# Another issue order for the first half of a fused attention and feed-forward kernel: values of the fourth pair ahead of the next batch's keys, zero fills moved

## The chip, the core and the metric

The kernel runs on one core of a Trainium2 chip. The core has five engines that run side by side and meet at semaphores: TensorE (PE, with PEld for its weight loads), VectorE (DVE), ScalarE (ACT), GpSimd (POOL) and SyncE (SP). SP mostly issues DMA transfers; ACT issues a few, and POOL issues some through a queue of its own. The metric is the device time of one launch in microseconds (us), lower is better.

## The reference, cut to what matters

```python
# q, k, v: (4 batches, 8 heads, 768 positions, 64)    is_retrieval = [1, 0, 1, 0, 0, 0, 1, 0]
scores = (1 / sqrt(64)) * q @ k.T
causal = rel >= 0                                      # rel = query position - key position
stream = causal & ((key < 4) | (rel < 64))             # 4 sink keys and a window of 64
scores = where(retrieval head ? causal : stream, scores, -1e9)
a = softmax(scores)
x = (a @ v) -> (3072 tokens, 512)                      # heads side by side
h = x @ w_in                                           # w_in: 512 x 2048
g = maximum(h, 0) + alpha * minimum(h, 0)
out = g @ w_out                                        # w_out: 2048 x 512
```

Inputs and output are float32. Three of the eight heads (0, 2, 6) are retrieval heads and see all earlier keys; five are streaming heads.

## The kernel before

The work is tiled by pairs of heads. `PAIRS` is (2, 6), (1, 5), (0, 4), (3, 7), so a batch has four pairs, and the sixteen pairs are numbered n = 0 to 15 (0 to 3 are batch 0, 4 to 7 batch 1, and so on). The feed-forward part works on token tiles t = 0 to 7: each batch is cut into a tile of 512 tokens (even t) and one of 256 (odd t).

The program is not ordered by loops. It defines some 1,070 small items by name, and the string `ORDER` (lines 14 to 71) lists all names once. The loop at line 817 runs them in that order. Each engine executes its own instructions strictly in the order in which they are issued, so `ORDER` fixes the order on PE, DVE, ACT, POOL and SP at once. The names, n being a pair:

- `Lq`, `Lk`, `Lv` n: DMA loads of queries, keys, values (L204 to L249), issued by SP. The buffers qf, kf and vf have four slots each, so pair n uses slot n modulo 4. Rows of queries and retrieval keys of the first two batches are read in long pieces (1,536 bytes, some keys 512); values are always read in rows of 256 bytes (L247, L249).
- `Cq`, `Ck`, `Cv` n: casts to bfloat16 (L320, L333, L348); the letters in `CQ`, `CK` and `CV` (L301 to L303) say on which engine. For n up to 5 most are on POOL. `Cv` of a pair with streaming heads adds copies of the sink rows (L311).
- `Tq`, `Tk`: transposes on PE into a PSUM bank (L363); `tq`, `tk`: copies from there to qT and kT (L368, L386 to L392). From n = 8 on DMA transposes `Dq`, `Dk` do this.
- `S` n.h.m: scores on PE (L411, L421, L428), `s`: their exponential on ACT (L467, L515, L521), `m`: mask factors on DVE. For n below 4 the mask is added on PE instead (L460, L499), with the tiles nmr and nms that POOL makes (items `nmr`, `nms`).
- `A` n.h: weights times values on PE (L554), `a`: division on DVE (L564, L565). `X`, `x`: the transposed result into xT (L579, L584; some by DMA, L573).
- `P` t.f: first feed-forward product (L599), with `p` the relu of the negated value on ACT (L604) and `g` the combination on DVE (L611), which frees the bank. For t = 0 and f below 6 the product comes in three parts, `P0.f.0` (pairs 0 and 1), `.1` (pair 2), `.2` (pair 3).
- `O` t.s.u: quarter u of the second product (L619), `o`: copy out and store (L625, L629). `wi` 0 to 7 and `wo` 0 to 3: the weight loads, issued by POOL (L707, L711). P0.4 and P0.5 need wi2 and wi3, P0.8 to P0.11 wi4 and wi5, P0.12 to P0.15 wi6 and wi7.
- `zero`, `one`, `kz`, `kfz`, `qz`, `vz`, `sz`, `nz`, `ro`, `so`, `vo`: constant fills (L293), on DVE, POOL or ACT (kz2).

PSUM has eight banks. `take` (L145) gives an item the allowed bank that was freed longest ago in the order of issue, `give` (L151) frees it, so the order of issue also decides which earlier item each bank's next user waits for.

Scores of pairs from 4 on are not issued at once: `S` items collect in `burst`, and `emit_burst` (L415) issues them before the next item that may not stand beside a burst (L432). If both heads have at least 576 columns in it, the two heads' matmuls are issued in turns on the two halves of the rows of the array (L428, 64 rows each), otherwise one after the other (L421).

At most eight transfers of SP's and ACT's queues are under way: each transfer waits for the one eight places before it. PE starts with `warm` matmuls on the identity.

Of the kernel before, what the change touches and what calls it, by code (L numbers as in the profile page):

```python
# [11 lines left out]


ORDER = """
Lq0.0 kz3 id zero Lk0 warm0 Ck0.1 qz0 Lk2 La Ck2.0 Lq0.1 vz3 nmr Cq0.0 Cq0.1 vz1 kz0 Lq1 Tq0.0 warm1 Lq2 kz2 Ck0.0
Ck2.1 qz Tk0.0 sz1 sz2 vz0 tq0.0 Cq1 Lk1 warm2 tk0.0 Tk0.1 Lv0 Ck1.0 Cq2 vo S0.0.0 s0.0.0 kz1 tk0.1 Ck1.1 S0.0.2
m6.0.2 Cv0 Tq0.1 m14.0.2 s0.0.2 Lk3 vz2 Tk2 S0.0.1 Lv1 tq0.1 Lq3 Tq1 s0.0.1 tq1 nms Lq5 Ck3.0 S0.1.1 tk2.1 Ck3.1
S0.1.2 Tk1 sz0 s0.1.1 tk2.0 Tq2 S0.1.0 A0.0 Cv1 tk1.0 s0.1.2 S1.0.0 s0.1.0 A0.1 S1.0.1 tq2 s1.0.0 s1.0.1 Lv2 Tk3 wi1
S2.1.1 wi0 so s2.1.1 tk1.1 wi2 S2.1.0 Lk4 a0.0 S1.1.1 s1.1.1 a0.1 X0 Cq3 A1.0 Cv2 Lv3 a1.0 Ck4.1 Lk5 s2.1.0 Cq5 S2.0.2
# [838 lines left out]
```

## Time and profile before

| | |
|---|---|
| median of 4 runs | 233.57 us (231.96 to 234.46) |
| profiled execution | 234.23 us, its span 232.5 us |
| PE busy | 223.1 us (96%), 1998 matmuls |
| DVE, ACT, POOL busy | 152.4, 139.0, 48.6 us |
| chain that ended last | PE 82%, DMA 10% (of these vf 9%), DVE 3% |
| DMA | 36.63 MB, 158 GB/s over the span |
| granted PE clock | 0.999 |

The chain of waits is followed back from the last instruction: at each step to what released it, or to the instruction before it on its engine. In the timeline, a bracket shows how long the engine stood idle before a row and what ended that. Times are counted from the start of the span. A busy PE is not PE at its peak, since matmuls overlap: four matmuls of 512 columns follow each other every 0.216 us (0.86 us for four in the chain), though one alone shows 0.38.

### The profile page before, as it was taken

The page shows a single profiled execution, that of the slowest core. Times are in us where ns is not written, and L with a number is a line of the kernel's source. Part 1 is how long each engine was busy: PE and PEld are TensorE (multiplying, and loading weights), DVE is VectorE, ACT ScalarE, POOL GpSimd, SP SyncE. Part 2 cuts the span into 40 slices and gives each one's busy share as a digit, 9 for nine tenths or more (in the row PEclk, how much of TensorE's full clock was granted, in tenths as well). Part 3 has the DMA queues.
Part 4 walks back from the last instruction along what each step waited for, and adds up shares of the span by engine and source line. Part 5 has one row for each costly group of instructions (what it writes and reads, how often), then busy time and mean ns, then how long its engine had stood idle before and what let it go on. Part 6 is the DMA issues. An engine that isn't in the chain of part 4 may idle for free.

```text
span 232.5 us, 5230 instructions
## 1 busy us (share of the span) xinstructions
PE 223.1 (96%) x1998; PEld 136.4 (59%) x1998; DVE 152.4 (66%) x393; ACT 139.0 (60%) x280; POOL 48.6 (21%) x97
## 2 busy tenths in 40 slices
PE   6989979999999999999999999999999999999994
PEld 5778847556556665665466445556854555554553
DVE  4695746898785865998997358979990345645110
ACT  5578727998698639736764874498522333623231
POOL 3679668001482004000001000010000020000000
PEclk9999999999999999999999999999999999999999
DMA  6989999999999699948989999894310130110033
GB/s 211 274 207 269 234 245 253 202 196 227 223 198 211 143 218 258 231 88 164 196 128 177 239 237 183 160 198 75 71 35 0 45 138 1 45 47 1 0 135 137
DMA packets 92449, 36.63 MB, mean 158 GB/s; under 512 B 79472, under 2 KB 90632, under 8 KB 92424
## 3 DMA queue, kind: packets, MB, share of 16 engines
q1 hardware_dynamic: 86168, 26.97, 56.4%
q0 software_dynamic: 5792, 8.93, 17.4%
q10 hardware_dynamic: 464, 0.40, 0.5%
q8 instruction: 15, 0.25, 0.5%
q14 instruction: 10, 0.08, 0.1%
HBM read 27.55 MB, written 6.29 MB: 146 GB/s over the span
## 4 chain that ended last, share of the span: by engine, by line
PE 82%; DMA 10%; DVE 3%; POOL 1%; SPq 1%; issue 1%; ACT 1%; POOLq 0%; ACTq 0%
PE P L619 35%; PE P L599 33%; DMA vf<-in_v_dram 9%; PE P L554 6%; PE P L428 4%; DVE g L611 2%; PE P L421 2%; PE P L638 2%; DMA kf<-in_k_dram 1%; PE P L579 1%; POOL vb L348 1%; PE P L363 1%; SPq L224 0%; DVE natm L333 0%; ACT neg L604 0%
## 5 line engine op out<-in xcount | busy, mean ns | idle before, releaser
L611 DVE SCALAR_TENSOR_TENSOR g<-neg,oma,P 128x512 bf16<-128x512 f32 (+1 forms) x128 | 72.9, 610 | 38.6 <-ACT neg L604 37.8
L599 PE MATMUL P<-xT,w_in_b 128*128 128x512 bf16 (+1 forms) x512 | 90.1, 326 | 0.0
L619 PE MATMUL P<-w_out_b,g 128*128 128x512 bf16 x368 | 87.6, 379 | 0.0
L604 ACT ACTIVATE neg<-P 128x512 f32<-128x512 f32 x96 | 54.8, 605 | 54.1 <-PE P L599 46.6
L599 PEld LDWEIGHTS <-w_in_b 128*128 128x128 bf16 x512 | 48.9, 98 | 32.2 <-issue 0.2
L619 PEld LDWEIGHTS <-g 128*128 128x128 bf16 x368 | 34.0, 98 | 36.0 <-issue 1.4
L467 ACT ACTIVATE eR<-P 128x448 bf16<-128x448 f32 (+6 forms) x63 | 36.0, 619 | 12.8 <-PE P L460 3.4
L629 POOL DMA_DIRECT2D out_dram<-ot x18 | 9.9, 550 | 127.1 <-ACT ot L625 127.1
L565 DVE TENSOR_TENSOR xn<-P,rcp 128x448 bf16<-128x448 f32 (+1 forms) x32 | 19.4, 608 | 1.1
L625 ACT COPY ot<-P 128x512 f32<-128x512 f32 x23 | 13.3, 595 | 9.1 <-PE P L619 6.7
L515 ACT ACTIVATE eS<-P 128x352 bf16<-128x352 f32 x30 | 13.7, 484 | 5.3 <-PE P L421 4.8
L521 ACT ACTIVATE eS<-P 128x384 bf16<-128x384 f32 (+1 forms) x25 | 13.3, 571 | 5.1 <-PE P L428 2.7
L554 PE MATMUL P<-vb,eS 128*128 128x65 bf16 x260 | 11.3, 193 | 1.7 <-POOL vb L348 1.6
L554 PEld LDWEIGHTS <-eS 128*128 128x128 bf16 x260 | 10.3, 97 | 4.5 <-issue 2.1
L564 DVE RECIPROCAL rcp<-P 128x7 f32<-128x7 f32 (+1 forms) x32 | 6.4, 199 | 8.5 <-PE P L554 8.3
L411 PE MATMUL P<-qT,kT 128*128 128x192 bf16 (+13 forms) x68 | 11.2, 250 | 0.8 <-DVE qT L368 0.8
L530 DVE TENSOR_TENSOR eS<-eS,ms_near 128x352 bf16<-128x352 bf16 x30 | 9.5, 335 | 2.6 <-ACT eS L515 2.4
L477 DVE TENSOR_TENSOR eR<-eR,mr_near 128x128 bf16<-128x128 bf16 (+5 forms) x36 | 7.0, 226 | 5.1 <-ACT eR L467 5.1
L348 POOL CAST vb<-vf 128x896 bf16<-128x896 f32 x6 | 5.6, 939 | 22.3 <-DMA vf<-in_v_dram 18.5
L554 PE MATMUL P<-vb,eR 128*128 128x65 bf16 x276 | 10.3, 192 | 0.0
L428 PE MATMUL P<-qT,kT 64*128 64x176 bf16 (+13 forms) x159 | 10.3, 251 | 0.0
L554 PEld LDWEIGHTS <-eR 128*128 128x128 bf16 x276 | 9.6, 97 | 1.0
(100 smaller groups left out, 186.2 us busy)
## 6 DMA issues: line engine op xcount, KB each, us to landing
out_dram<-ot POOLq DMA_DIRECT2D x18, 256.0 KB, 3.6
vf<-in_v_dram SPq DMA_DIRECT2D x22, 192.0 KB
kf<-in_k_dram SPq DMA_DIRECT2D x21, 192.0 KB
qf<-in_q_dram SPq DMA_DIRECT2D x18, 192.0 KB
qf<-in_q_dram SPq DMA_DIRECT2D x7, 384.0 KB
w_in_b<-in_moe_w_in_dram POOLq DMA_DIRECT2D x8, 256.0 KB, 8.8
w_out_b<-in_moe_w_out_dram POOLq DMA_DIRECT2D x4, 512.0 KB, 11.3
kf<-in_k_dram SPq DMA_DIRECT2D x9, 196.0 KB
```

Of the source, the lines that this page charges most:

```text
L411: nc.tensor.matmul(to, keys, queries, start=True, stop=stop)
L428: nc.tensor.matmul(to, keys[own], queries[own], start=True, stop=True)
L467: nc.scalar.activation(ebuf[n, hh][:, lo:hi].rearrange("p (x c) -> p x c", x=len(parts)), P[:, got[0]:got[0] + len(parts), 0:(hi - lo) // ...
L515: nc.scalar.activation(slots, sc[:, 0:352].rearrange("p (s c) -> p s c", c=176), AF.Exp, scale=scale)
L521: nc.scalar.activation(slots, sc.rearrange("p x (s c) -> p x s c", c=192), AF.Exp, scale=scale)
L554: nc.tensor.matmul(pav[:, i, :], e[:, o:o + 128], vv[:, j, hh, 0:D + 1], start=(m == 0), stop=(m == len(terms) - 1))
L565: nc.vector.tensor_tensor(xn[n][:, 0:nt, D * hh:D * hh + D], pav[:, :, 0:D], rcp.to_broadcast([128, nt, D]), op=ALU.mult)
L599: nc.tensor.matmul(psg[:, w * i:w * (i + 1)], w_in_b[:, c, 128 * fb:128 * (fb + 1)], xT[:, c, o:o + w], start=(x == 0), stop=(x == 3))
L604: nc.scalar.activation(neg[t, f], bank(held["P", t, f][0]), AF.Relu, scale=-1.0)
L611: nc.vector.scalar_tensor_tensor(g_buf[t % 2][:, fb, 0:w], neg[t, f][:, c], oma[:, fb:fb + 1], bank(got[0])[:, c], op0=ALU.mult, op1=ALU.add)
L619: nc.tensor.matmul(bank(held["O", t, s][0]), g_buf[t % 2][:, f, 128 * s:128 * (s + 1)], w_out_b[:, f, :], start=(f == 0), stop=(f == 15))
L625: nc.scalar.copy(ot, bank(got[0]))
```

## The change

Only `ORDER` changes, and only up to the middle: the same names, each once, stand in another order up to `A8.1` and `A9.1` (pairs of batch 2); behind them the string is the same. On every engine the number of instructions of each kind stays, but for the score matmuls, whose bundles are cut at other places.

What moves on the queues:
- SP: before, the loads went `Lk1 Lv0 Lk3 Lv1 Lq3 Lq5 Lv2 Lk4 Lv3 Lk5 Lq4 Lk6 Lq6 Lk7 Lv7 Lv4 Lk8 Lq7 Lv5 Lq8 Lk9 Lv6 Lq9`; after, `Lk1 Lv0 Lq2 Lk2 Lk3 Lv1 Lq3 Lv2 Lq5 Lv3 Lk4 Lk5 Lq4 Lk7 Lq6 Lk6 Lq7 Lv5 Lq8 Lk9 Lk8 Lv4 Lq9 Lv6`, with Lv7 behind `Dk8.1 Dq8 Dk8.0`. Lk2 was third and is now behind Lq2.
- POOL: before, `kz3 id Ck0.1 Ck2.0 nmr Cq0.1 Ck2.1 Cq1 Ck1.0 Cq2 Ck1.1 Cv0 nms Ck3 Cv1 wi1 wi0 wi2 Cq3 Cv2 Ck4.1 Cq5 wi3 wi6 wi7 Ck4.0 nz1 Cv3 wi5 Ck5.0 kfz2 wi4 Ck5.1 Cq4 ...`; after, `id nmr nms Ck0.1 Cq0.1 Cq1 kz3 Ck1 Cv0 Cq2 Ck2 Ck3.0 kfz0 Ck3.1 Cv1 wi0 wi1 Cq3 wi2 Cv2 Cq5 Cv3 wi3 wi6 Ck4.0 Ck4.1 wi7 wi4 wi5 Ck5.1 wo1 nz0 nz1 Ck5.0 wo0 Cq4 ...`.
- PE: `A3.0` now comes ahead of `S3.1 X2 Tk4 Tq5`, and `A3.1` behind them; the parts of P0 and P1 are interleaved in another way, and so are the bundles of scores of pairs 4 to 9.
- DVE: the fills `sz1 vz1 kz0 vo zero vz0` stand ahead of `Cq0.0`.

```diff
 ORDER = """
-Lq0.0 kz3 id zero Lk0 warm0 Ck0.1 qz0 Lk2 La Ck2.0 Lq0.1 vz3 nmr Cq0.0 Cq0.1 vz1 kz0 Lq1 Tq0.0 warm1 Lq2 kz2 Ck0.0
-Ck2.1 qz Tk0.0 sz1 sz2 vz0 tq0.0 Cq1 Lk1 warm2 tk0.0 Tk0.1 Lv0 Ck1.0 Cq2 vo S0.0.0 s0.0.0 kz1 tk0.1 Ck1.1 S0.0.2
-m6.0.2 Cv0 Tq0.1 m14.0.2 s0.0.2 Lk3 vz2 Tk2 S0.0.1 Lv1 tq0.1 Lq3 Tq1 s0.0.1 tq1 nms Lq5 Ck3.0 S0.1.1 tk2.1 Ck3.1
-S0.1.2 Tk1 sz0 s0.1.1 tk2.0 Tq2 S0.1.0 A0.0 Cv1 tk1.0 s0.1.2 S1.0.0 s0.1.0 A0.1 S1.0.1 tq2 s1.0.0 s1.0.1 Lv2 Tk3 wi1
-S2.1.1 wi0 so s2.1.1 tk1.1 wi2 S2.1.0 Lk4 a0.0 S1.1.1 s1.1.1 a0.1 X0 Cq3 A1.0 Cv2 Lv3 a1.0 Ck4.1 Lk5 s2.1.0 Cq5 S2.0.2
-wi3 Lq4 s2.0.2 S1.1.0 s1.1.0 ro Lk6 Tq3 x0 tq3 S2.0.0 wi6 A1.1 S2.0.1 s2.0.0 wi7 A2.1 tk3.0 s2.0.1 a1.1 Ck4.0 nz1 Cv3
-tk3.1 S3.0.0 S3.0.1 wi5 s3.0.1 s3.0.0 A2.0 a2.1 Tq5 Ck5.0 a2.0 Tk4 S3.1.1 kfz2 Lq6 s3.1.1 wi4 X1 x1 tq5 S3.1.0 X2
-s3.1.0 idf x2 A3.0 tk4.0 tk4.1 Lk7 a3.0 P0.2.0 A3.1 P0.1.0 Al P0.1.1 P0.3.0 P0.2.1 a3.1 X3 Ck5.1 P0.3.1 x3 al Lv7 Lv4
-P0.0.0 P1.0 P0.2.2 p0.2 P1.4 P0.1.2 p1.4 Cq4 P1.6 P0.3.2 g0.2 P0.0.1 Tk5 p0.1 p0.3 g1.4 g0.1 p1.6 tk5.0 g1.6 kfz3
-P0.0.2 p0.0 g0.3 wo0 g0.0 P0.5.0 P1.2 tk5.1 P0.6 p0.6 p1.0 Tq4 P0.13 P0.5.1 P0.4.0 p1.2 g0.6 nz0 p0.13 P0.4.1 wo1 tq4
-g1.0 P0.14 g1.2 P0.5.2 g0.13 P1.8 Ck6.1 p0.5 P0.10 Cq6 p1.8 p0.14 P0.4.2 g0.5 Lk8 p0.4 Tq6 Ck6.0 kfz0 tq6 P0.9 Lq7
-P0.11 wo3 g1.8 p0.9 g0.14 kfz1 mr p0.10 wo2 g0.4 g0.9 S4.1.3 S4.0.0 S5.0.0 g0.10 S4.1.4 s4.1.3 P0.7 P0.8 s4.0.0 P1.14
-p0.11 s4.1.4 p0.8 s5.0.0 Lv5 Cv4 p1.14 S4.1.2 S4.0.4 g0.11 s4.1.2 g0.8 ms P0.15 S4.1.1 s4.0.4 S5.1.2 p0.15 S5.0.2
-S4.0.5 g1.14 s5.1.2 P0.12 g0.15 O0.0.0 p0.7 p0.12 P1.10 s4.1.1 s4.0.5 s5.0.2 g0.7 m4.0.5 m5.1.2 Lq8 Cv5 P1.12 S5.1.0
-S4.0.3 S4.1.0 S4.0.1 g0.12 s4.0.3 O0.3.0 one m5.0.0 m4.0.0 O0.1.0 m4.1.4 Ck7.1 O0.0.1 O0.0.2 ns s5.1.0 p1.10 s4.1.0
-S4.0.2 s4.0.1 m4.0.4 g1.10 m4.0.1 S5.1.1 S4.1.5 m4.0.3 S5.0.1 s5.1.1 m4.1.1 Lk9 s4.1.5 O0.1.1 O0.0.3 Ck7.0 s5.0.1
-m4.1.3 Tk6 m5.1.1 s4.0.2 p1.12 o0.0 Cv7 Ck8 Tk7 A4.0 Cq7 m4.1.5 g1.12 Lv6 m5.1.0 tk6.1 O0.3.1 m5.0.1 Tq7 O0.3.2 m4.0.2
-Lq9 tk6.0 tk7.0 Cq8 S6.0.1 S6.0.0 m5.0.2 tq7 A5.1 nr Dk8.1 a5.1 O0.1.2 a4.0 A5.0 O0.1.3 s6.0.1 tk7.1 m4.1.0 o0.1
-S6.1.0 S6.1.2 S6.0.2 S6.0.4 a5.0 s6.1.2 Dq8 O0.3.3 m6.1.2 S7.1.2 s6.0.4 s6.0.0 s6.1.0 Dk8.0 O0.2.0 s6.0.2 S7.1.0 o0.3
-S6.0.3 S6.0.5 S7.1.1 S6.1.1 Ck9 s7.1.0 O0.2.1 s7.1.2 O0.2.2 Cv6 m6.0.0 s7.1.1 X5 m7.1.0 A4.1 s6.1.1 S8.1.1 x5 s6.0.5
-S7.0.2 s6.0.3 m6.0.5 S8.1.5 m6.0.4 S7.0.0 S8.1.4 S7.0.1 m6.0.1 m6.1.1 Dk9.0 m7.1.1 s7.0.1 m6.0.3 s7.0.0 Lv9 O0.2.3
-A6.0 Cq9 m7.1.2 s8.1.1 s8.1.5 O1.1.0 a6.0 a4.1 s8.1.4 Dq9 O1.1.1 s7.0.2 m6.1.0 m7.0.0 A7.1 S8.0.0 S8.1.2 S8.1.0 S8.0.1
-A6.1 s8.0.0 m7.0.1 m7.0.2 m8.1.1 O1.1.2 s8.0.1 Dk9.1 a6.1 X4 A7.0 a7.0 s8.1.0 X6 a7.1 O1.0.0 O1.0.1 O1.1.3 x6 Lv8 X7
-S8.0.3 S9.0.1 Lq10 s8.1.2 Lq11 s9.0.1 Cv9 near1 S9.1.1 x7 O1.0.2 m8.1.0 o0.2 s8.0.3 O1.0.3 S9.1.2 S8.1.3 m8.1.4 S8.0.4
-S9.0.2 o1.1 S9.1.0 m8.1.5 S9.0.0 s9.1.1 s8.1.3 s8.0.4 P2.6 Cv8 p2.6 Lk11 o1.0 m8.1.3 Lk10 P2.5 p2.5 P2.14 s9.1.2 P3.0
-s9.1.0 s9.0.2 p2.14 P2.3 P2.7 Lq12 g2.6 Lq13 m9.1.0 p2.3 g2.5 s9.0.0 near0 m10.0.2 near2 A8.1 p3.0 g2.14 g2.3 g3.0
-Cq11 p2.7 m9.1.1 m8.0.4 P2.0 p2.0 g2.7 P2.8 Lk12 g2.0 P2.2 p2.8 m9.1.2 S8.0.5 P2.13 p2.2 A9.1 Lk13 m8.0.1 g2.2 s8.0.5
-m9.0.0 P3.14 P2.15 p2.13 g2.8 Ck11 P3.8 p2.15 P2.9 a8.1 g2.15 P3.4 P2.1 a9.1 P3.10 Ck10 p3.4 Dk10.0 g2.13 P2.11 p2.1
-...
+sz1 vz1 Lq0.0 id La Lk0 Lq0.1 kz0 Lq1 vo zero vz0 warm0 Cq0.0 kz1 nmr Lk1 Lv0 nms m14.0.2 kz2 Ck0.1 Cq0.1 Lq2 Tq0.0
+Cq1 qz0 kz3 Lk2 warm1 Ck1.0 Ck0.0 Tk0.0 tk0.0 ro Ck1.1 warm2 Cv0 tq0.0 Tk0.1 Lk3 S0.0.1 vz3 S0.0.0 Tq0.1 Cq2 s0.0.1
+Tq1 sz2 tk0.1 s0.0.0 tq1 S0.0.2 tq0.1 idf Tk1 Lv1 S0.1.2 vz2 s0.0.2 s0.1.2 S0.1.1 A0.0 Ck2.0 s0.1.1 tk1.0 Ck2.1 qz sz0
+tk1.1 S0.1.0 s0.1.0 Ck3.0 kfz0 S1.0.1 so Ck3.1 Tq2 Tk2 Lq3 A0.1 s1.0.1 Cv1 tq2 wi0 S1.0.0 one wi1 Cq3 tk2.1 s1.0.0
+a0.0 wi2 S2.1.0 S1.1.1 Tk3 tk2.0 s2.1.0 s1.1.1 Lv2 S2.1.1 S2.0.2 a0.1 s2.1.1 X0 S1.1.0 s2.0.2 tk3.0 tk3.1 s1.1.0 Lq5
+A1.0 Lv3 x0 Cv2 S2.0.0 Lk4 s2.0.0 a1.0 Tq3 A1.1 S2.0.1 tq3 A2.1 a1.1 S3.0.0 Cq5 s2.0.1 a2.1 S3.0.1 Lk5 Cv3 Lq4 X1
+s3.0.0 x1 s3.0.1 wi3 A2.0 A3.0 a2.0 wi6 S3.1.1 Ck4.0 a3.0 S3.1.0 X2 Ck4.1 Tk4 wi7 s3.1.1 Tq5 wi4 s3.1.0 A3.1 x2 Al
+P0.0.0 a3.1 P0.1.0 wi5 X3 al P0.3.0 Ck5.1 P0.1.1 tk4.0 P0.3.1 Lk7 tq5 x3 wo1 tk4.1 P0.1.2 P0.0.1 nz0 P0.2.0 nz1 P1.0
+P0.2.1 P0.2.2 p1.0 P0.3.2 P0.4.0 p0.1 p0.3 P1.4 Ck5.0 g1.0 g0.1 p0.2 Tk5 wo0 P0.0.2 tk5.0 g0.3 Lq6 Cq4 Lk6 P1.6 g0.2
+wo2 Tq4 p1.6 P0.6 P0.13 g1.6 p1.4 P1.2 p0.6 g0.6 g1.4 tk5.1 p0.0 P0.7 p0.13 P0.4.1 P0.14 g0.0 tq4 P0.5.0 P0.5.1 p1.2
+P0.5.2 g0.13 p0.14 p0.5 g1.2 g0.5 Cq6 P0.4.2 P1.8 Lq7 P0.10 Tq6 p1.8 g0.14 P0.9 g1.8 p0.10 m6.0.2 tq6 p0.4 P0.11 g0.10
+P0.8 g0.4 p0.9 p0.11 Lv5 P1.14 p0.8 S5.0.2 S5.1.2 S4.1.2 g0.9 p0.7 Lq8 g0.11 S4.0.4 P0.15 s5.0.2 S4.1.4 g0.8 S4.0.0
+s4.1.2 p1.14 g0.7 p0.15 s4.0.4 g1.14 P0.12 O0.0.0 Ck7.0 S4.1.1 S4.0.1 s5.1.2 g0.15 s4.0.0 S4.0.5 p0.12 S4.1.3 P1.12
+s4.0.1 s4.1.1 O0.0.1 Ck6.1 Ck6.0 kfz1 ms P1.10 wo3 p1.12 s4.1.4 s4.0.5 S5.0.0 Ck7.1 Cv5 O0.0.2 g1.12 m5.1.2 s4.1.3
+g0.12 S5.0.1 S4.1.0 S4.0.2 p1.10 Lk9 S4.0.3 s5.0.0 m5.0.0 S5.1.1 Lk8 S5.1.0 Cq7 O0.0.3 s5.1.0 Lv4 m5.1.0 s5.0.1 Tk7
+s4.0.3 O0.1.0 Tq7 s5.1.1 m5.0.1 Cv4 mr g1.10 O0.3.0 tk7.0 tk7.1 Tk6 m5.1.1 A5.1 s4.1.0 O0.1.1 tq7 O0.1.2 tk6.1 O0.1.3
+m5.0.2 Cq8 a5.1 kfz3 s4.0.2 Ck8 ns m4.0.0 Lq9 tk6.0 S6.1.0 S4.1.5 o0.0 S6.0.1 S7.0.0 m4.0.3 m4.1.3 S7.1.0 S6.0.0
+m4.0.4 O0.3.1 Lv6 Dk8.1 o0.1 m4.0.5 s6.1.0 s7.1.0 m4.1.0 m4.0.1 A5.0 Dq8 a5.0 Dk8.0 s7.0.0 O0.3.2 A4.0 s4.1.5 s6.0.0
+O0.3.3 O1.1.0 o0.3 Ck9 m4.1.5 S6.1.2 S6.0.5 a4.0 S6.0.2 m6.1.0 S6.0.4 s6.0.1 S6.1.1 Lv7 S7.1.1 X5 s6.1.2 s6.1.1 s6.0.4
+s6.0.5 Dk9.0 Dk9.1 s7.1.1 m4.1.1 Cv6 m6.0.0 m6.0.4 s6.0.2 O1.0.0 O1.0.1 S8.1.1 x5 S8.1.4 S7.0.2 S7.0.1 m7.0.0 m6.0.1
+m4.1.4 m7.1.1 S7.1.2 S6.0.3 m6.0.5 Cq9 O1.1.1 s7.1.2 A4.1 Dq9 m6.1.2 m6.1.1 s6.0.3 O1.1.2 A6.1 s7.0.1 a4.1 m6.0.3
+s7.0.2 m7.1.2 A6.0 s8.1.1 s8.1.4 m7.0.2 Lk11 m7.0.1 Cv7 O0.2.0 S8.1.5 O0.2.1 m7.1.0 A7.1 A7.0 m10.0.2 a6.1 a7.0 X4
+O1.1.3 O0.2.2 S8.0.1 m4.0.2 O0.2.3 nr s8.1.5 s8.0.1 S9.1.2 a7.1 S9.0.1 S9.0.0 S8.1.2 Lq11 o1.1 S8.1.0 a6.0 S8.0.0
+s9.0.0 O1.0.2 Lv9 s8.1.0 s9.1.2 X6 Ck11 near0 s9.0.1 X7 x6 Lv8 x7 m8.1.0 O1.0.3 s8.1.2 m8.1.5 S8.0.3 S9.1.0 m8.1.4
+S9.0.2 m9.1.2 s8.0.0 o0.2 m8.0.1 S8.0.4 S8.1.3 S8.0.5 S9.1.1 o1.0 s9.0.2 s8.1.3 Lq12 P2.7 m9.0.0 m8.1.1 P2.8 s8.0.4
+kfz2 P2.14 p2.7 P2.5 p2.8 s9.1.1 s8.0.3 s9.1.0 m9.1.1 p2.14 P3.0 P2.2 g2.8 g2.7 Lk10 Lq13 p3.0 g2.14 P2.3 m8.1.3 Lq10
+m8.0.4 P2.6 P2.0 g3.0 p2.2 g2.2 Cv9 m9.1.0 Cq11 p2.3 P3.14 P2.13 near1 Lk13 Cv8 g2.3 p2.5 p2.0 p2.6 g2.5 P2.15 Lk12
+A8.1 p2.13 g2.6 s8.0.5 g2.0 near2 P3.8 A9.1 p2.15 P2.9 a8.1 g2.15 P3.4 P2.1 a9.1 P3.10 Ck10 p3.4 Dk10.0 g2.13 P2.11
+...
 """.split()
```

## The prediction

> **What bounds the kernel now.** I read the page first, then the stretches, the chain of waits, the timelines of TensorE, POOL and ScalarE, and last what the DMA engines moved. The median is 233.57 us; the profiled execution took 234.23 us with a span of 232.5, so 1.7 us lie outside the span. The changes below are worked out on that execution and put on the median.
>
> ```profile
> 0.00:30.30 30.30, 24.50 (x366) 21.57 (x367) 20.10 (x53) 21.67 (x29) 20.67 (x41) 1.00 0.98 240
> 30.30:48.50 18.20, 17.98 (x147) 11.15 (x147) 13.31 (x29) 12.68 (x27) 7.96 (x16) 1.00 1.20 228
> 48.50:88.30 39.80, 39.80 (x403) 23.22 (x403) 30.10 (x89) 30.11 (x70) 11.32 (x25) 1.00 1.05 203
> ```
>
> After the window the columns are its length, then busy PE, weight loads, DVE, ACT, POOL, the granted clock, DMA share and GB/s. From 30.3 us on TensorE is busy without a hole: in its timeline every piece starts where the one before ends. What comes later costs nothing unless it opens a hole, and all that can be won lies before 30.3 us, where PE is busy 24.5 of 30.3. The clock is granted in full.
>
> ```profile
> 20.30 8.88 DMA vf<-in_v_dram
> ...
> 29.32 0.94 POOL vb L348
> ...
> 30.32 0.35 POOL vb L311
> ...
> 30.71 0.49 PE P L554 x11
> ```
>
> In the chain, Lv3 (values of the last pair of batch 0) decides when the filled part begins: it lands at 29.2, POOL casts it (Cv3) and copies sinks, and A3.0 starts.
>
> ```profile
> 28.20 0.55 PE L579 MATMUL P<-ident,xn 128*128 128x128 bf16 x7
> 30.30 0.22 PE L554 MATMUL P<-vb,eS 128*128 128x65 bf16 x2 [1.55 <-POOL vb L348]
> 30.71 0.49 PE L554 MATMUL P<-vb,eS 128*128 128x65 bf16 x11 [0.18 <-POOL vb L311]
> ```
>
> PE waits 1.55 + 0.18 us for it. Lv3 waits in turn on the DMA engines, from its issue at 18.84 to 20.80 on.
>
> ```profile
> 16.00:18.00 2.00, 2.00 (x46) 2.00 (x44) 1.90 (x7) 2.00 (x4) 1.16 (x2) 1.00 0.94 320
> ...
> 22.00:26.00 4.00, 4.00 (x82) 3.48 (x80) 3.42 (x10) 3.35 (x6) 3.94 (x8) 1.00 1.20 185
> 43.00:52.00 9.00, 8.97 (x61) 5.06 (x60) 8.46 (x20) 8.89 (x18) 0.00 (x0) 1.00 1.22 197
> ...
> 59.00:61.00 2.00, 2.00 (x16) 0.83 (x15) 1.11 (x6) 0.23 (x2) 0.06 (x1) 1.00 1.31 235
> ```
>
> Loads of queries (rows of 1536 bytes) run at 320 GB/s and more, values alone (256 bytes) at 235, and values beside POOL's weight loads share 185 to 197.
>
> **Part one: Lv3 in front of Lk4.** SP's bytes up to the end of Lv3 fall by Lk4's 384 KB; Lq5 only changes places with Lv2. In the trace the queue reaches Lk4 at 20.0 us and is through it at 21.2; after the change it reaches Lv3 there. From then to 22.0, at the 780 rows a us that the DMA records show for Lv2, about 1,400 of Lv3's 1,584 rows are over. The rest meets w_in: the first bytes of POOL's loads, issued from 18.74, appear at 21.3, and in 22 to 25 us the records show 76, 53 and 117 value rows a us beside 134 to 171 w_in rows. The rest then takes to about 24.3; with the half us between last byte and semaphore, Lv3 lands at 24.8 instead of 29.2 (bounds 23.6, when POOL is free for it, and 27).
>
> A rule speaks against this. The Trainium skill, "DMA: Bandwidth & Descriptors", section "Queues, rings and completion order", says that a DMA engine takes turns between the queues that have work for it, a packet of descriptors from each, so a load of short rows gets few bytes beside one of long rows. The trace agrees where both run: at 43 to 52 us the records are 152 rows of 256 bytes to 152 of 1024 a us, or 39 GB/s against 155. If turns were taken from Lv3's first row, its 396 KB would need 10 us, it would land at 30.7 and nothing would be won. I take 24.8 because the same records show 633 value rows in 21 to 22 us against 33 of w_in: most of Lv3 passes before w_in has begun.
>
> **Part two: what POOL and PE do next.** In POOL's new order wi3, wi6, Ck4.0 and Ck4.1 stand behind Cv3, and on PE Tk4 and Tq5 stand in front of A3.1. From POOL's rows: cast and copies 1.65 us, two w_in issues 1.25, the two key casts 0.95, a handover 0.1, then 12 transposes on PE 0.66. A3.1 begins 4.6 us after the landing, at 29.4. PE's own work would let it start a little earlier (A3.0 0.39, S3.1 1.0, X2 0.4 behind A3.0), and ACT's last exponentials of pair 3 are over by then: Cq3 now has two w_in issues in front of it, not three (0.64 us earlier), and that pair's scores come earlier with it. Before, A3.1 starts at 31.31 with P0.2.0 (0.43) already done, which is like 30.88. Won: **1.5 us** (2.7 to a loss of 0.7 at the bounds).
>
> **Part three: w_in comes later.** wi3 and wi6 were issued at 24.05 and 24.65 and are now issued from 26.45; wi7 follows behind Ck4.1.
>
> ```profile
> w_in_b<-in_moe_w_in_dram POOLq DMA_DIRECT2D x8, 256.0 KB, 8.8
> ```
>
> P0.4.0 needs wi3, and stands 5.15 us behind A3.1 (39 + 16 + 43 + 43 + 49 + 43 + 3 x 22 + 22 + 43 + 88 + 3 x 22 hundredths), at 34.55. With the 6.6 us that wi1 took in an empty queue wi3 lands at 33.05, with the page's 8.8 at 35.25: 0 to 0.7, I take **0.3**. The others have more room: wi7 is needed 9.1 us behind A3.1, wi4 and wi5 13.8, at a spacing of 1.9 us a load. w_out, on the same queue, is needed from 51 us; the third and fourth loads landed at 51.9 and 55.3 before and are wanted at 55.3 and 57.
>
> **Part four: fills and masks.** The sink mask (1.46 us on POOL) moves ahead of the first key cast. `zero`, which it needs, comes after 1.3 us of fills on DVE, at 2.2; nmr 0.82 and the mask end at 4.5, and that cast waits for its load until 4.59 anyway. kz3 (0.84) goes behind Cq1, where POOL waited 0.91. DVE's fills ahead of Cq0.0 end at 2.4 and its load lands at 3.86. I cost all fills at nothing: they lie in front of the PE wait that remains at A3.0 (about 1 us); without that cover the sink mask would cost its 1.46.
>
> **Part five: the middle.** The scores of batch 1 are bundled differently: 27 bundles for 30, and 8 matmuls go from the plain to the paired form. Columns to stream fall from 26,570 to 26,033; at 0.216 us for 512 columns that is **0.23 us** won. But they come in larger bundles, of up to 16 matmuls and 7 banks, and PE, which is in order, waits for the last release. Before, that just fitted:
>
> ```profile
> 65.35 0.79 ACT L386 COPY kT<-P 64x768 bf16<-64x768 bf16 x1
> ```
> ```profile
> 66.20 0.56 PE L421 MATMUL P<-qT,kT 128*128 128x314 bf16 x3
> ```
>
> The key copy tk6.0 ends at 66.14 and the first scores of pair 6 start at 66.20. ACT had waited 1.00 and 1.77 us for PE earlier in that stretch. In the new order the bundle (S4.1.5, S6, S7) needs tk6.0 too, and its last matmuls the bank that o0.0 empties. PE reaches it 34.1 us behind A3.1. ACT starts its first relu (p1.0) 4.7 us behind A3.1, as before, and until tk6.0 is through it has all 24 relus (0.50 us apart), 17 exponentials (0.43 to 0.55), Cq6, Cq7, tq4, tq6, tq7 and five key copies: 28.5 us of work and, by the order in which PE feeds it, 1.2 to 1.8 us of waits. So tk6.0 comes at 34.4 to 35.0 and o0.0 half a us later: 0.3 to 1.0, I take 0.9. In the same way, from each bank's previous user: the bundle behind O0.0.0 0.2, the one behind O0.0.2 (waits for s5.0.0) 0.2, the one behind O1.0.1 0.2, the one behind O0.2.3 (a6.0 is the last of four outputs on DVE) 0.2, the bundle of 7 banks behind O1.0.3 (its last part waits for o0.2) 0.3. Sum **2.0** (0 to 3). DVE keeps ahead: its 24 prelus at 0.66 to 0.79 are never the last by more than 0.3 us. Lk8, Lv4 and Lv7 go behind other loads on SP, Lv7 behind two transposes; from the rates above Lk8 lands near 61 and DVE asks for it near 62.5, Lv7 at 74 against 78. I cost those at nothing; each us that Lk8 is later than 62.5 would hold DVE's queue, the masks of pair 4 in it. From A8.1 on the order is the old one.
>
> **Sum.** -1.5 + 0.3 - 0.23 + 2.0 = +0.6: 234.2 us.
>
> **Rivals.**
> First, the holes don't come. For it: ACT had 2.8 us of waits in that stretch that a better order can fill. Against: they were waits for PE, and the larger bundles release the exponentials later. 233.57 - 1.5 - 0.23 + 0.3 = 232.1; with the early landing too (23.6: 2.7 won, w_in in time) 230.6, which is over 1% faster.
> Second, slower: Lv3 meets w_in with more rows left. A queue that reaches Lv3 0.8 us later leaves some 600 rows more to the crowded stretch, and it lands at 27. Then A3.1 starts at 31.6 (+0.7), wi3, issued at 28.65, lands at 37.45 by the page's 8.8 and is wanted at 36.75 (+0.7); with 2.0 - 0.23 that is +3.2 and 236.8. It decides from a landing of about 26.4.
> Third, the order does nothing that can be measured at the front because PE's older work fills the wait: then only the middle counts, +1.8, 235.4. PE's idle rows before 30 us speak against it.
>
> **How the numbers follow.** Likeliest case 0.50 at 234.2; the first rival 0.22, half of it at 230.6; the second 0.20; the third 0.08. A measurement of this kernel tells about 1% (2.3 us; its runs lie from 231.96 to 234.46) from no change. Faster 0.11; slower 0.20 and the upper part of the likeliest and the third case, 0.26; within 1% 0.63. The range from 231.5 to 236.8 leaves out the early landing and little above the second rival.
>
> **What would show it.** Right: the wait of A3.0 for vb gone or under 1 us, Cv3 near 25, A3.1 near 29.4, and later waits of PE on tk6.0, o0.0 or a6.0 that were not there. Wrong: Cv3 past 26.5, a wait of L599 for w_in_b over 0.7, a DVE wait for kf near 62, or no hole in PE from 48 to 88 us.

## The result and the profile after

The changed kernel takes 231.78 us (median of 39 runs, 230.75 to 233.43), the kernel before 234.38 us (58 runs, 231.94 to 242.15). The ratio is 0.992 with a 95% interval of 0.9903 to 0.9937: it is faster, by 0.6 to 1.0%. The ratio leaves out some executions of the old program that took much longer; what happened in executions like them is one of the findings below. The forecast was 234.2, 0.6 us slower than before, so the sign was wrong.

The profiled execution of the changed kernel took 233.00 us with a span of 231.3, near the long end of its own runs; the span is 1.2 us shorter than before. The same three stretches as before (columns: length, then busy PE, weight loads, DVE, ACT, POOL, the granted clock, DMA share and GB/s):

```profile
0.00:30.30 30.30, 25.55 (x389) 22.30 (x390) 21.60 (x56) 20.71 (x27) 21.19 (x44) 1.00 1.01 238
30.30:48.50 18.20, 18.03 (x129) 10.63 (x126) 12.30 (x24) 14.42 (x29) 7.22 (x12) 1.00 1.20 227
48.50:88.30 39.80, 39.52 (x410) 22.95 (x409) 28.50 (x94) 31.59 (x74) 11.74 (x27) 1.00 1.07 201
```

PE now does 25.55 us of work in the first 30.3 us where it did 24.50. In the third stretch it is no longer full: 39.52 of 39.80, one hole of 0.28. Its timeline shows the front. The bracket is the idle time before a row and what ended it:

```profile
25.71 0.22 PE L554 MATMUL P<-vb,eS 128*128 128x65 bf16 x2 [0.38 <-POOL vb L348]
26.11 0.49 PE L554 MATMUL P<-vb,eS 128*128 128x65 bf16 x11 [0.18 <-POOL vb L311]
...
29.33 0.51 PE L363 MATMUL P<-ident,natm 128*128 128x128 bf16 x6 [1.33 <-POOL natm L333]
29.67 0.50 PE L363 MATMUL P<-ident,natq 128*128 128x128 bf16 x6
30.01 0.56 PE L554 MATMUL P<-vb,eS 128*128 128x65 bf16 x13
...
65.38 0.83 PE L428 MATMUL P<-qT,kT 64*128 64x314 bf16 x12 [0.28 <-ACT kT L386]
```

A3.0 starts at 25.71 instead of 30.30 and waits 0.38 + 0.18 us. A new wait of 1.33 us stands at Tk4, for the keys of pair 4. A3.1 starts at 30.01; before it started at 31.47 with 0.43 us of P0.2.0 already done, so 1.03 us are won. In POOL's timeline the cast of Lv3 begins when its load lands, and that of the keys as well:

```profile
24.72 0.93 POOL L348 CAST vb<-vf 128x896 bf16<-128x896 f32 x1 [1.38 <-DMA vf<-in_v_dram]
25.72 0.63 POOL L311 COPY vb<-vb 4x192 f32<-4x192 f32 x2
26.30 1.23 POOL L707 DMA_DIRECT2D w_in_b<-in_moe_w_in_dram  x2
27.50 0.54 POOL L333 CAST natm<-kf 128x384 bf16<-128x384 f32 x1
28.76 0.51 POOL L333 CAST natm<-kf 128x384 bf16<-128x384 f32 x1 [0.72 <-DMA kf<-in_k_dram]
```

From the same later piece of PE to the same piece (P2.9, and everything behind it), the changed kernel is 0.72 us ahead: 1.03 won at A3.1, then 0.28 at the bundle of pairs 6 and 7 and 0.17 at Tk5 lost, and the remaining +0.14 is put down to the bundles' gain (0.23 by the prediction's columns) less smaller gaps, which was not measured apart. Another 0.5 us comes from the very end (last section).

### The profile page after: what moved, and what is told of

Read it like the earlier page. It is cut to its first block, busy times and chain, and to the rows that moved or that the text cites. A ratio compares the mean times of both kernels' runs of the same rounds, so it can differ in the third digit from the quotient of the medians.

```text
span 231.3 us, 5237 instructions
## 1 busy us (share of the span) xinstructions
PE 223.2 (97%) x1998; PEld 135.9 (59%) x1998; DVE 150.8 (65%) x393; ACT 140.0 (61%) x280; POOL 48.4 (21%) x97
## 4 chain that ended last, share of the span: by engine, by line
PE 82%; DMA 7%; ACT 4%; DVE 2%; POOL 2%; issue 1%; SPq 0%; POOLq 0%; ACTq 0%
PE P L599 33%; PE P L619 32%; DMA kf<-in_k_dram 5%; PE P L554 5%; PE P L428 4%; DMA qf<-in_q_dram 2%; PE P L702 2%; PE P L638 2%; PE P L421 1%; DVE kT L390 1%; PE P L363 1%; ACT eR L467 1%; POOL natk L293 1%; PE P L579 1%; ACT eS L521 1%
## 5 line engine op out<-in xcount | busy, mean ns | idle before, releaser
L619 PEld LDWEIGHTS <-g 128*128 128x128 bf16 x368 | 34.0, 98 | 35.1 <-issue 1.4
L467 ACT ACTIVATE eR<-P 128x448 bf16<-128x448 f32 (+6 forms) x63 | 36.7, 620 | 14.3 <-PE P L421 5.6
L554 PEld LDWEIGHTS <-eS 128*128 128x128 bf16 x260 | 10.2, 97 | 3.0 <-issue 1.4
L411 PE MATMUL P<-qT,kT 128*128 128x192 bf16 (+13 forms) x68 | 11.1, 250 | 0.7 <-DVE qT L368 0.4
L428 PE MATMUL P<-qT,kT 64*128 64x176 bf16 (+16 forms) x167 | 10.7, 250 | 0.3 <-ACT kT L386 0.3
L428 PEld LDWEIGHTS <-kT 64*128 64x128 bf16 x167 | 6.6, 94 | 6.9 <-issue 5.7
```

The lines of the kernel that those rows point to most:

```text
L411: nc.tensor.matmul(to, keys, queries, start=True, stop=stop)
L428: nc.tensor.matmul(to, keys[own], queries[own], start=True, stop=True)
L467: nc.scalar.activation(ebuf[n, hh][:, lo:hi].rearrange("p (x c) -> p x c", x=len(parts)), P[:, got[0]:got[0] + len(parts), 0:(hi - lo) // ...
L554: nc.tensor.matmul(pav[:, i, :], e[:, o:o + 128], vv[:, j, hh, 0:D + 1], start=(m == 0), stop=(m == len(terms) - 1))
L619: nc.tensor.matmul(bank(held["O", t, s][0]), g_buf[t % 2][:, f, 128 * s:128 * (s + 1)], w_out_b[:, f, :], start=(f == 0), stop=(f == 15))
```

## The experiments

In all kernels of this section only the string `ORDER` differs from one of the two kernels, unless a diff shows code. It has one line less there, so line numbers are one lower than in the kernels above. "before" next to a median is the kernel before on the same chip.

### The front alone, and the middle alone

```diff
 # e1: changed order up to A3.1, behind it the order of before
+sz1 vz1 Lq0.0 id La Lk0 ... Lv3 x0 Cv2 S2.0.0 Lk4 ... Tq5 wi4 s3.1.0 A3.1
 P0.2.0 P0.1.0 Al P0.1.1 P0.3.0 P0.2.1 a3.1 X3 Ck5.1 ...
 # e2: order of before up to A3.1, behind it the changed order
```

> The changed order up to A3.1, and behind it the order of before. Theory (the gain comes from the front): A3.1 starts near 30.0 us as in the changed kernel, every later piece of PE about 1.0 us earlier than before, time 0.9 to 1.4 us under before (ratio 0.994 to 0.996). Rival (the gain comes from the other bundles of scores and the order in the middle): no gain, ratio 0.999 to 1.001.

> The order of before up to A3.1, and behind it the changed order. Theory: bundles win 0.23 us, holes of 0.3 to 0.5 us give it back, so within 0.4 us of before (ratio 0.998 to 1.002), with a hole of PE at the bundle of pairs 6 and 7 of some 0.3 us. What the prediction said of the middle: 2.0 us of holes less 0.23, ratio 1.006 to 1.009. Rival (the middle brings the gain): ratio 0.993 to 0.996.

e1: 233.17 us against 236.11 of before, ratio 0.990 (0.985 to 0.996). e2: 235.43, ratio 0.996 (0.991 to 1.002). The front alone brings the gain, as far as these intervals can tell; the middle alone brings none that can be measured, and does not cost the 0.6 to 0.9% that the prediction gave it. PE's hole at the bundle of pairs 6 and 7 is 0.28 us in e2, as in the changed kernel. The traces agree: from the start of A3.1 to the end of p2.9 it is 76.4 us in before and in e4 (P0.2.0's 0.43 added), 76.7 in the changed kernel and 76.3 in e6, which is the changed kernel again. In e1 a wait for weights shows, as the prediction's third part had it (0.3), since the old middle asks for its weights sooner:

```profile
33.75 2.55 PE L598 MATMUL P<-xT,w_in_b 128*128 128x256 bf16 x19 [0.42 <-DMA w_in_b<-in_moe_w_in_dram]
```

The profile of e2 (its longest execution, 239.35 us) held a surprise. Its front is the old one, instruction for instruction, and yet POOL's cast of Lv3 begins at 33.82, not at 29.32:

```profile
33.82 0.93 POOL L347 CAST vb<-vf 128x896 bf16<-128x896 f32 x1 [6.86 <-DMA vf<-in_v_dram]
```

### The two loads alone

```diff
 # e3: the changed kernel, Lv3 and Lk4 changed back
-A1.0 Lv3 x0 Cv2 S2.0.0 Lk4 s2.0.0
+A1.0 Lk4 x0 Cv2 S2.0.0 Lv3 s2.0.0
 # e4: the kernel before, Lv3 ahead of Lk4, and what needs the keys behind what needs the values
-S2.1.0 Lk4 a0.0 ... Cv2 Lv3 a1.0 Ck4.1 Lk5 ... a1.1 Ck4.0 nz1 Cv3 ... Tk4 S3.1.1 ... A3.0
+S2.1.0 Lv3 a0.0 ... Cv2 Lk4 a1.0 Lk5 ... a1.1 nz1 Cv3 Ck4.0 Ck4.1 ... S3.1.1 ... A3.0 Tk4
```

> The changed kernel with the two loads Lv3 and Lk4 back in the old order on SP, nothing else. Theory (the earlier landing of Lv3 makes the front's gain): Cv3 waits until about 28 to 29.5 instead of 24.7, A3.0 follows it at about 29.5 to 31, and the time is 1.0 to 3 us above the changed kernel, so no faster than before (ratio 0.997 to 1.005). Rival (fills and the earlier start of A0.0 make it): within 0.3 us of the changed kernel, ratio 0.991 to 0.994.

> The kernel before with Lv3 ahead of Lk4, both key casts Ck4 on POOL behind Cv3, and Tk4 behind A3.0 so that nothing in front of Cv3 or A3.0 needs the keys; fills and the rest as before. Theory: Lv3 lands near 25, A3.0 starts when PE is through its older work, about 27.5 to 28.5, A3.1 waits for Tk4 and so for Lk4 near 30, and the time is 0.5 to 1.5 us under before (ratio 0.994 to 0.998). Rival (fills and early start decide): no gain, ratio 0.999 to 1.001; and if POOL's weight loads now meet Lv3 the landing is at 27 or later.

e3: 237.56 us, ratio to before 0.997 (0.990 to 1.004), where e1 on the same chip had 0.990; its six executions lie between 234.02 and 239.8, those of e1 between 232.36 and 235.11. With two names changed back no gain is left that can be measured; the two intervals overlap, and what shows the cause is the trace. e4: 234.21, ratio 0.992 (0.985 to 0.999). Five names moved in the old kernel bring a gain like that of the whole change. PE in e3 (the profiled execution, 238.89, is one of the longer ones; Cv3 begins at 29.99):

```profile
30.98 1.17 PE L553 MATMUL P<-vb,eS 128*128 128x65 bf16 x13 [5.44 <-POOL vb L347]
```

In e4, Cv3 begins at 26.12 (expected near 25), A3.0 does not wait, and the issue of the output's last copy ends at 228.30, as in e1 (228.22). e4 has the old fills and starts A0.0 at 15.18, e1 at 12.17: the fills and the 3 us of earlier start are worth nothing that shows, as the fourth part said.

### When does Lv3 land in the old order?

These four are the unchanged kernel before.

> The kernel before once more, for one look at where Lv3 lands in another execution of the same program. Theory (Lv3's landing in the old order depends on how many of its rows have passed when the first rows of w_in arrive, which differs from execution to execution): Cv3 starts anywhere from 29 to 34 us, later than 29.3 more often than not, and the time follows it one to one. Rival (it lands at 29.3 and the late landings of the runs before this one came from their edits): Cv3 within 0.5 us of 29.3.

> The kernel before, unchanged, one of three more looks. Theory (Lv3's landing in the old order varies between executions): among the three, Cv3 starts at 31 us or later in at least one, with PE waiting 3 us or more before A3.0, and that execution is longer than the others by as much or more; none of them starts Cv3 before 28. Rival (it always lands near 29, and the spread of times comes from elsewhere): Cv3 at 28.3 to 29.8 in all three.

> As the run before it, the second of three looks at the unchanged kernel before: Cv3 at 31 us or later in at least one of the three by the theory, at 28.3 to 29.8 in all by the rival.

> As the two runs before it, the third look at the unchanged kernel before: Cv3 at 31 us or later in at least one of the three by the theory, at 28.3 to 29.8 in all by the rival.

e9 alone (Cv3 at 28.51, earlier than both expectations) decided nothing. The next three did: 32.38, 31.65 and 31.05. PE's wait in e13 and in e15:

```profile
33.36 1.16 PE L553 MATMUL P<-vb,eS 128*128 128x65 bf16 x13 [5.58 <-POOL vb L347]
```
```profile
32.04 0.22 PE L553 MATMUL P<-vb,eS 128*128 128x65 bf16 x2 [3.76 <-POOL vb L347]
```

So the 29.32 on which the prediction was built is one draw, and an early one. The late three ran on one chip, but of 17 other executions of the same kernel there only five had a clock clearly under full (0.976 to 0.993; theirs 0.984 to 0.991, told in the last section), so it is not the chip alone. The DMA records say why. For each run, when some 25 rows of w_in had gone (single rows come up to 0.7 us earlier), how many of Lv3's 1,584 rows were still to come then, and when its last row passed:

| run | order of the loads | w_in begins | rows of Lv3 left | last row of Lv3 | Cv3 begins |
|---|---|---|---|---|---|
| before | Lk4, Lv3 | 21.8 | 966 | 28.5 | 29.32 |
| e9 | Lk4, Lv3 | 21.3 | 815 | 27.7 | 28.51 |
| e14 | Lk4, Lv3 | 21.4 | 1,051 | 30.9 | 31.65 |
| e15 | Lk4, Lv3 | 20.5 | 1,584 | 30.5 | 31.05 |
| e13 | Lk4, Lv3 | 20.1 | 1,584 | 31.8 | 32.38 |
| e2 | Lk4, Lv3 | 21.6 | 1,584 | 33.2 | 33.82 |
| e4 | Lv3, Lk4 | 20.5 | 792 | 24.8 | 26.12 |
| changed kernel | Lv3, Lk4 | 21.6 | 151 | 24.0 | 24.72 |
| e6, the same again | Lv3, Lk4 | 21.4 | 175 | 24.1 | 24.68 |

About a microsecond on either queue decides whether some 800 or all rows of Lv3 meet w_in: from e14 to e15 w_in comes 0.9 us earlier and Lv3's first row 1.0 us later. An earlier landing further ahead can bring this about: in e13 and e15 POOL casts Lv1 at 15.91 and 15.82 (17.15 in the first profile of before), and so issues its first w_in at 17.49 and 17.40 (18.74). The rule that the prediction weighed (the Trainium skill, "DMA: Bandwidth & Descriptors", section "Queues, rings and completion order": a DMA engine takes turns between queues that have work) gave an estimate of 10 us (at the 39 GB/s read at 43 to 52 us) for a Lv3 that meets w_in from its first row. e13, e15 and e2, in the old order, show 11.5, 8.9 and 11.1 us from its first row to its last. In the changed kernel nine tenths of the load are through before w_in begins; in e4, where half is, the rest still passes in 4.3 us.

### Lv3 without w_in beside it

```diff
 # e5: the kernel before, no weight load ahead of Cv3
-Cv1 ... Tk3 wi1 S2.1.1 wi0 ... wi2 ... wi3 ... wi6 ... wi7 ... Cv3
+Cv1 ... Tk3 S2.1.1 ... Cv3 wi1 wi0 wi2 wi3 wi6 wi7
```

> The kernel before with all its weight loads wi0, wi1, wi2, wi3, wi6, wi7 on POOL behind Cv3, so that no row of w_in is under way while Lv3 is; loads on SP as before (Lk4 ahead of Lv3). Theory (Lv3 is late because its short rows meet w_in): Lv3 passes at some 780 rows a us right behind Lk4, Cv3 starts at 23 to 24.5 instead of 29.3 to 33.8, and A3.0 does not wait for it; the first products of w_in then wait for their weights, with 6.6 to 9.6 us from issue to landing from about 32 to 35 us, so the time is 1 to 4 us above before. Rival (the place behind Lk4 on SP is what makes it late): Cv3 at 27 us or later.

With Lk4 still ahead of it, Lv3's last rows pass in the microsecond from 24.0, and 681 of them start in the one from 22.0. Cv3 begins at 26.41, later than expected, but without a wait: POOL was busy with what stands ahead of it, and PE does not wait for A3.0. So it is w_in and not the place behind Lk4 that made it late. The price was dearer than the 1 to 4 us expected: 242.54 us in the one execution, against 237.2 of before, since the first product then waits for its weights:

```profile
37.49 1.01 PE L598 MATMUL P<-xT,w_in_b 128*128 128x512 bf16 x2 [8.89 <-DMA w_in_b<-in_moe_w_in_dram]
```

### ScalarE at the bundle of pairs 6 and 7

```diff
         copy, small = (cast_of(x) for x in ("AA" if n >= 4 else "VV"))
...
+        if n == 6:
+            copy(slots[:, 0:6, a:last, :], src[:, first:z, :].rearrange("d (j m) t -> d j m t", j=6))
         copy(slots[:, 0:6, a:last, :], src[:, first:z, :].rearrange("d (j m) t -> d j m t", j=6))
```

> The changed kernel with one copy of ScalarE doubled: the key copy tk6.1 runs twice, some 0.8 us more on ScalarE ahead of tk6.0. Theory (ScalarE is at the edge at the bundle of pairs 6 and 7, and PE waits for it one to one): the hole of PE there grows from 0.28 to about 1.05 us, and the time behind it by 0.8. Rival (the hole is not set by ScalarE's amount of work): it stays under 0.6.

```profile
65.65 0.53 PE L429 MATMUL P<-qT,kT 64*128 64x314 bf16 x9 [1.10 <-ACT kT L385]
```

The hole grew from 0.28 to 1.10, by the 0.8 us of the copy, and nothing behind it takes that back: from the start of the bundle to the end of p2.9 it is 41.36 us in e10 and in e6. The mechanism of the fifth part stands: PE waits for tk6.0, and ScalarE has no slack in front of it. Its size did not.

### What else held A3.1

e6 is the changed kernel again, for comparison on one chip; e7 and e8 move the transposes that wait for the keys.

```diff
 # e7 (and e8, which goes on with the middle of before)
-S3.1.0 X2 Ck4.1 Tk4 wi7 s3.1.1 Tq5 wi4 s3.1.0 A3.1 ... X3
+S3.1.0 X2 Ck4.1 wi7 s3.1.1 wi4 s3.1.0 A3.1 ... X3 Tk4 Tq5
```

> The changed kernel once more, to be compared with the next two on one chip. Theory: Cv3 at 24 to 25, within 1.5 us of the other execution; ratio 0.990 to 0.994. Rival (the earlier Lv3 is one draw of a landing that varies in both orders): Cv3 at 27 or later.

> The changed kernel with the transposes Tk4 and Tq5 of PE behind X3 instead of ahead of A3.1, so that A3.1 does not wait for Lk4 and the cast Ck4.1. Theory (that wait is what kept part two from its 1.5 us): A3.1 starts at 28.3 to 28.7, when the exponentials of pair 3 are over, instead of 30.0, and the time is 0.6 to 1.4 us under the changed kernel. Rival (another wait takes its place: w_in wi3, or tk6.0 on ScalarE, which has the same work behind A3.1): under 0.4 us.

> The same front as the run before this one (changed order with Tk4 and Tq5 behind X3), and behind it the middle of the kernel before. Theory (the two middles cost the same within 0.5 us, the old one with a wait for w_in of 0.4 instead of one for tk6.0): within 0.6 us of the run with the changed middle. What the prediction said: the old middle is better by 1.8 us less a wait for w_in of 0.3 to 1.0, so 0.8 to 1.5 us faster than it.

e6: 231.66 us against 237.2 of before (0.978, 0.971 to 0.986; on this chip the kernel before took longer than elsewhere, the changed one did not). e7: 231.29, 0.4 under e6 and inside its own scatter (230.9 to 232.66): nothing won that can be measured. My theory of that wait fell. In e6 the wait at Tk4 is only 0.55, and in e7 another one of the same size stands in its place, the exponentials of pair 3:

```profile
29.11 0.57 PE L553 MATMUL P<-vb,eS 128*128 128x65 bf16 x13 [0.57 <-ACT eS L520]
```

e8: 233.26, 2.0 above e7, where the prediction had the old middle faster by 0.8 to 1.5. In the trace 0.9 of it lies ahead of the last copy, 0.70 of that a wait for a key copy of pair 4, and 0.3 in the tail told below. The rest, some 0.7, is not accounted for.

### A shorter front

```diff
 # e12
-Cv3 Lq4 X1 ... wi3 A2.0 A3.0 a2.0 wi6 S3.1.1 Ck4.0 a3.0 S3.1.0 X2 Ck4.1 Tk4 ... Tq5 ... A3.1 ... X3
+wi3 Cv3 Lq4 X1 ... A2.0 S3.1.1 S3.1.0 A3.0 a2.0 wi6 Ck4.0 a3.0 X2 Ck4.1 ... A3.1 ... X3 Tk4 Tq5
 # e16: e12, and on POOL
-wo1 tk4.1 P0.1.2 P0.0.1 nz0 P0.2.0 nz1 ... Ck5.0
+tk4.1 P0.1.2 P0.0.1 P0.2.0 ... Ck5.0 wo1 nz0 nz1
```

> The changed kernel with the scores S3.1 ahead of A3.0 (PE does them while the values are on their way), Tk4 and Tq5 behind X3, and the load wi3 ahead of Cv3 on POOL, which is idle there. Theory (what holds A3.1 is the chain from the scores of pair 3 over ScalarE's exponentials, which stood behind A3.0's wait): no wait of A3.0, A3.1 at 27.6 to 28.3 instead of 29.1 to 30.0, time 0.6 to 1.5 us under the changed kernel. Rival (the next wait takes it: w_in behind A3.1, or wi3's rows on the way of Lv3): within 0.5 us of it or above.

> The run with S3.1 ahead of A3.0, and on POOL the weight load wo1 and the fills nz0 and nz1 (2.5 us together) behind the cast Ck5.0 instead of ahead of it. Theory (a front gain reaches the end one to one if no later wait takes it): Tk5 waits under 0.3 us instead of 1.60, and the time is 0.9 to 1.6 us under the changed kernel, near 230.3. Rival (the transfers are what holds pair 5's keys, or ScalarE and the banks give it back in the middle): Tk5 waits over 1 us, or the hole at the bundle of pairs 6 and 7 grows by over 0.8; within 0.5 us of the changed kernel.

e12: 231.68 us (ratio to before 0.992, 0.988 to 0.996). A3.1 starts at 27.70, 1.5 to 2.4 us earlier than in the changed kernel (0.67 of that are the transposes that now stand behind it), and nothing of it arrives: Tk5 takes it, which waits for a cast that stands behind two fills and a weight load on POOL.

```profile
27.70 0.55 PE L553 MATMUL P<-vb,eS 128*128 128x65 bf16 x13 [0.56 <-DVE xn L564]
...
36.61 0.51 PE L362 MATMUL P<-ident,natm 128*128 128x128 bf16 x6 [1.60 <-POOL natm L332]
```

e16 clears POOL: Tk5's wait is gone. But its median is 231.76 (ratio 0.989, 0.986 to 0.993), and in its profile Cv3 begins only at 26.36, so A3.1 starts at 29.20. Neither beats the changed kernel.

## Why the prediction was wrong

**What bounds the kernel: right, but its time was a draw.** Lv3 decided when PE's filled part began. That it landed at 29.2 was taken as a property of the kernel; its cast begins anywhere from 28.5 to 32.4 in five executions of the kernel before, and at 33.8 in e2, which has the same front.

**Part one: right.** 24.8 was forecast for Lv3; Cv3 begins at 24.72, and at 24.68, 25.40 and 25.63 in e6, e10 and e11, which have the same front. "Most of Lv3 passes before w_in has begun": 82 to 304 of 1,584 rows were left when some 25 rows of w_in had gone.

**Part two: right in mechanism.** A3.1 was to start at 29.4, 1.5 us won (before, it started at 31.47 and not at the 31.31 that the working used, so 1.6 by its own terms); it started at 30.01 in the first profile, and at 29.18, 29.89 and 30.13 in the others. Not foreseen was the wait of Tk4 for Lk4 (0.54 to 1.33), which the new order puts ahead of A3.1; but e7 shows that the exponentials of pair 3 end at almost the same time.

**Part three: small, and near nothing.** 0.3 was forecast for w_in (the terms of its 5.15 add up to 5.18, which changes nothing). None in the changed kernel's first profile and e6, 0.20 in e11, 0.42 in e1. The weight loads took longer than the 8.8 us used (9.6 by the changed kernel's page) and still came in time, since the changed order asks for them later.

**Part four: right** (e4 against e1).

**Part five is the step that failed.** "Sum 2.0 (0 to 3)": the hole at the bundle of pairs 6 and 7 was 0.28 where I took 0.9, and of the five others, 1.1 us together, none shows. ScalarE's last rows before it and the chain are as described there:

```profile
54.02 0.99 PE P L599 x8
...
55.10 0.60 ACT neg L604
...
63.16 0.77 ACT kT L390
...
64.10 0.54 ACT eR L467
64.64 0.69 ACT kT L386
65.33 0.05 issue
65.38 0.82 PE P L428 x10
```

tk6.0 ended 35.3 us behind A3.1 (forecast 34.4 to 35.0), and PE reached the bundle at 65.10, 35.1 behind it (forecast 34.1). In e6 the two are 34.9 and 34.7. Both sums were short, PE's by 0.6 to 1.0 us, and the term was their difference. They also began at the wrong place. The chain above shows it: ScalarE last waited for PE at p1.12 (55.10), so all that came before has no part in the hole. From there ScalarE works without a wait to the end of tk6.0, 10.2 us, and PE without a wait to the bundle, 10.0 us. In all eight profiles with the new middle and the old copies the bundle starts 10.27 to 10.28 us after p1.12 with a hole of 0.28, though A3.1 starts anywhere from 27.7 to 36.6; in e10 it is 11.10. So the hole was a fixed property of the order. The term was mis-sized, not the mechanism (e10). For the other five, priced from each bank's previous user at 0.2 or 0.3, PE's timeline has no hole; that mechanism did not show at all.

With 0.28 for 2.0, and nothing for w_in, the prediction's own sum is -1.5 - 0.23 + 0.28 = -1.45, or 232.1: the first rival, to which it gave a chance of 0.22. The measured 231.78 lies between its two times, in part by luck: A3.1 came 1.0 us earlier in the first profile and 1.9 in e6 where 1.5 was forecast, the end of the program brought 0.5 that was not forecast at all, and the kernel before took 234.38 in the longer measurement where the sum began at 233.57. The second rival, the slower one, had the right mechanism and price (Lv3 meets w_in with more rows left) in the wrong kernel: the old order pays it, in the executions where Lv3 is late.

## What to carry to other kernels

A landing time read from one execution can be one draw of a race between two queues: count how many rows of the load are left when the other queue's first rows arrive, and look at more than one execution before a change is priced against it. A hole of one engine behind another is to be priced from the last place where the other one waited for it (10 us ahead here), and not as the difference of two sums of 35 us, which is not known to within its own size. Five further holes, priced at 0.2 to 0.3 each on the word of an order of issue, did not show, and should not have been added up as if each were certain. A shorter front reaches the end only if the next load behind it is early too.

## What the runs showed of the hardware that was not expected

**A late load costs PE almost twice.** In e13 A3.0 starts 3.06 us later than in the first profile of before, but the span is 5.6 us longer (238.1 to 232.5); in e14 it is 2.33 and 4.7, in e15 1.74 and 3.3. The stretches of e13 show where the rest goes (columns as above; the granted clock is the third number from the end):

```profile
28.00:30.00 2.00, 0.00 (x0) 0.00 (x0) 0.37 (x1) 1.78 (x3) 0.00 (x0) 1.00 1.23 219
30.00:32.00 2.00, 0.00 (x0) 0.00 (x0) 0.00 (x0) 0.00 (x0) 0.00 (x0) 1.00 1.16 239
32.00:34.00 2.00, 0.51 (x7) 0.39 (x7) 0.00 (x0) 0.00 (x0) 1.56 (x4) 0.61 1.11 319
34.00:36.00 2.00, 1.78 (x25) 1.45 (x24) 0.83 (x2) 0.00 (x0) 2.00 (x6) 0.50 1.12 349
36.00:38.00 2.00, 2.00 (x8) 0.57 (x6) 0.83 (x2) 0.00 (x0) 2.00 (x5) 0.50 1.32 209
38.00:40.00 2.00, 2.00 (x13) 1.15 (x12) 0.39 (x1) 0.00 (x0) 2.00 (x4) 0.68 1.38 174
```

PE stands idle for 5.58 us, the clock falls to half and stays there until about 39. Busy time by missing clock is 0.2 + 0.9 + 1.0 + 0.6 = 2.7 us, which is about the rest of the 5.6. The Trainium skill, "TensorE: Matmul & The Clock Gate", section "Part 1: The HAM clock gate", says that PE goes to half rate after an idle window of about 3.4 us whose place is not tied to the program. The runs agree: during or soon after waits of 3.76, 4.05, 5.44, 5.58, 6.22 and 8.89 us the clock was 0.50, after those of 1.5 us in the first profile of before and in e9 it was not; none between was seen. By stretches of 1 us, the clock fell 0.9 us before the end of the wait in e13 and 1.4 us after it in e15, and stayed at half for 3.4 us in e15 and for 6.8 us in the other five. The changed kernel's waits, 1.33 us at most, keep clear of it: in its first 39 executions and the four of e6 the clock over the span was 0.998 or more, and none took over 233.43 us. Of 50 executions of the kernel before whose clock is on record with the experiments, 18 had 0.976 to 0.993, and they took 235.9 to 242.0 us.

**A block of code in front of the last store.** In all nine profiles with the old middle it takes 2.5 to 3.0 us from the end of the last copy's issue on ScalarE to the end of the span; in all nine with the new middle 2.2. That is half a microsecond of the gain, in a part of the program that the change doesn't touch. The DMA records show an 8,192-byte transfer of the instruction queue at that place. Before, it runs from 230.37 to 230.93, and the last eight rows of the last store start only when it has ended, and are through at 231.12; in the changed kernel it runs from 230.43 to 230.96, behind the store's last row at 229.97. In number of instructions the two kernels' traces differ only in those that handle semaphores, on VectorE (463 and 458 instructions in all), ScalarE (390 and 401), SyncE (216 and 214) and, by one or two, on the others. Whose block it is was tried for VectorE:

```diff
         got = held.pop(("L", x))
+        if x == 0:
+            for _ in range(6):
+                nc.vector.memset(ms5[0:NSINK, 1, 148:152], 0.0)
         if not last:
```

> The changed kernel with six tiny fills on VectorE ahead of l0, near the end, where VectorE has over 6 us of idle time. Theory (the 8 KB block of code that is loaded at the end is VectorE's, and five instructions fewer on VectorE moved its load from ahead of the last store to behind it): the block is loaded ahead of the last rows of the store again, and from the end of the last copy's issue to the end of the span it is 2.5 to 3.0 us instead of 2.1 to 2.2. Rival (it is another engine's block): 2.1 to 2.2 stays.

The tail stayed at 2.2 us with the block behind the store, which speaks against VectorE. Whose block it is, and whether its place alone makes the half microsecond, stays open.
